# Attention in head pairs with transposed scores, and an MLP whose matmuls are issued between the attention phases

## The chip, the cores and the metric

The kernel runs on one core of a Trainium2 chip. The metric is the device time of one execution in microseconds (us), the median of three runs.

## The reference, cut to what matters

Attention over q, k, v of shape 8 batches x 8 heads x 576 positions x 64, then an MLP on the 4608 resulting tokens of width 512 with a hidden width of 2048.

```python
q_d, k_d, v_d = (t.reshape(B, H, 144, 4, D).mean(axis=3) for t in (q, k, v))
out_up = np.repeat(sm_attn(q_d, k_d, v_d), 4, axis=2)      # softmax over 144 groups
scores = np.where(np.abs(pos[:, None] - pos[None, :]) < 4, q @ k.T / 8, -1e9)
out_local = softmax(scores) @ v                            # a band of 7 positions
x = (out_up + out_local).transpose(0, 2, 1, 3).reshape(4608, 512)
h = x @ w_in                                               # 512 -> 2048
out = (h * sigmoid(h)) @ w_out                             # 2048 -> 512
```

## The kernel before

The program has two blocks, one after the other. The first does the attention, one head at a time, 64 times. Five engines each run a list of their own in order, tied together by counted semaphores (`Edge`). GpSimd (`g_D`, L442) loads q and k of two heads by a DMA that converts to bf16; SyncE (`sp_V`, `sp_W`, L449 to L460) loads v twice, once in plain rows and once in the five windows of the band. TensorE's list for a head is `pe_T` (transposes of q and k, L193 to L201; averages over groups of four by a matmul with `G_bf`, L206 to L222), `pe_D` and `pe_Dd` of the head before (transposing the normalised weights P, L256 to L268), `pe_S` and `pe_Sd` (scores, queries on the output's partitions, L236 to L244), `pe_O` and `pe_Od` of the head before (weights times v, L281 to L290). ScalarE does the exponentials (L305, L306, L314) and half of the copies out of PSUM (L324, L331, L353); VectorE multiplies by the band mask and sums each row (L377), takes reciprocals, scales the weights (L387), copies, and adds the two attention results into `xT` (L418, L423), which holds all 4608 tokens as 128 x 4 x 4608 in f32.

The second block begins when the last head is in `xT`. For each of nine groups of 512 tokens, `gemm1` makes 16 tiles of the hidden layer, four 128x512 matmuls each (L691), into two PSUM tiles; ScalarE takes the sigmoid (L676, SBUF), VectorE multiplies it by the PSUM tile (L650) into `gT` in bf16, and this frees the PSUM tile. `gemm2` of the group before follows as one run of 64 matmuls (L706); VectorE copies each of its four outputs (L659) and SyncE stores it.

A tile of `gemm1` may begin only when the tile two steps ago has been multiplied:

```python
eMG.wait(t, gch - 1)
```

Of the kernel before, what the change touches and what calls it, by code (L numbers as in the profile page):

```python
# [17 lines left out]
NCH = 5
QB = [0, 120, 240, 360, 480]  # L20
NQ = [120, 120, 120, 120, 96]
SK0 = [0, 117, 237, 357, 448]
MASK_IDX = [0, 1, 1, 1, 2]
MASK_OFF = [0, -3, -32]
# [2 lines left out]
NEG = -1.0e9


class Edge:  # L30

    def __init__(self, kctx, nc, name, dma=False):
        self.sem = kctx.enter_context(nc.semaphore(name))
        self.step = 16 if dma else 1
        self.n = 0

    def inc(self, inst):
        inst.then_inc(self.sem, self.step)
        self.n += 1
        return self.n  # L40

    def wait(self, eng, k):
        if k >= 1:
            eng.wait_ge(self.sem, self.step * k)  # L44


def bass_hourglass_attn__then__act_silu_kernel(
# [11 lines left out]
    with kctx:
        E = kctx.enter_context  # L60

        xT = E(nc.sbuf_tensor("xT", [128, 4, NTOK], F32))
# [12 lines left out]
        eDK = [edge(f"dk{i}", dma=True) for i in range(2)]
        eDV = [edge(f"dv{i}", dma=True) for i in range(2)]
        eDW = [edge(f"dw{i}", dma=True) for i in range(2)]
        eTq = edge("tq")
        eTk = edge("tk")
        ePvd = edge("pvd")  # L80
        ePs = edge("ps")
        ePsd = edge("psd")
        ePd = edge("pdg")
        ePdd = edge("pdd")
        ePo = edge("po")
        ePod = edge("pod")
        eDv = edge("dvcast")
        eXq = edge("xq")
        eXk = edge("xk")
# [34 lines left out]
        G64_bf = pa(nc.sbuf_tensor("G64_bf", [128, 16], BF16))
        Gf = pa(nc.sbuf_tensor("Gf", [128, 32], F32))
        w_out_st = pa(nc.sbuf_tensor("w_out_st", [128, 16, 512], F32))
        qkst = [pa(nc.sbuf_tensor(f"qkst{i}", [128, 9, 2 * D_], BF16)) for i in range(2)]
        vst = [pa(nc.sbuf_tensor(f"vst{i}", [128, 5, D_], F32)) for i in range(2)]
        wbst = [pa(nc.sbuf_tensor(f"wbst{i}", [128, NCH, D_], F32)) for i in range(2)]
        vbf = [pa(nc.sbuf_tensor(f"vbf{i}", [128, 5, D_], BF16)) for i in range(2)]  # L130
        wbf = [pa(nc.sbuf_tensor(f"wbf{i}", [128, NCH, D_], BF16)) for i in range(2)]
        qT_sb = [pa(nc.sbuf_tensor(f"qT{i}", [D_, S_], BF16)) for i in range(2)]
        kT_sb = [pa(nc.sbuf_tensor(f"kT{i}", [D_, S_], BF16)) for i in range(2)]
        qdT_sb = [pa(nc.sbuf_tensor(f"qdT{i}", [D_, SD], BF16)) for i in range(2)]
        kdT_sb = [pa(nc.sbuf_tensor(f"kdT{i}", [D_, SD], BF16)) for i in range(2)]
        P_sb = [pa(nc.sbuf_tensor(f"P{i}", [120, 640], BF16)) for i in range(2)]
# [609 lines left out]
```

## Time and profile before

| | |
|---|---|
| median of 3 runs (lowest to highest) | 718.29 us (716.72 to 719.34) |
| span of the profiled execution, first to last instruction | 715.0 us |
| median less that span | 3.3 us |
| busy: TensorE matmul, weight load | 623.9 us, 394.2 us |
| busy: VectorE, ScalarE, GpSimd | 452.8, 306.7, 71.4 us |
| attention block, to the first MLP matmul | 402.6 us |
| MLP block | 312.4 us |

For the profiled execution the page has the span and no other time; what lies around it is read as the 3.3 us by which the median is longer. A busy TensorE is not one at its peak: its matmuls overlap, and the share says nothing of the clock.

### The profile page before, as it was taken

The numbers are of one execution on the slowest core, as the hardware profiler recorded it, in microseconds if no ns is written. First come the engines' busy times: TensorE is split into PE (matmuls) and PEld (weight loads), VectorE is DVE, ScalarE is ACT, GpSimd is POOL, SyncE is SP. The second block draws the span as 40 slices with busy tenths as digits, with TensorE's granted clock in tenths as the row PEclk, the third lists the DMA queues.
The fourth block names the chain that finished last, engine by engine and source line by source line (L and its number), as shares of the span: only waits on it lengthen the run. The fifth ranks groups of instructions, "written<-read, shape, count | busy, mean of one in ns | idle before, by whom it ended". The sixth has DMA issues, their size and how long they took to land. (4 is left out here: it accounts for less than half of the span.)

```text
span 715.0 us, 12541 instructions
## 1 busy us (share of the span) xinstructions
PE 623.9 (87%) x3887; PEld 394.2 (55%) x3904; DVE 452.8 (63%) x1979; ACT 306.7 (43%) x978; POOL 71.4 (10%) x92
## 2 busy tenths in 40 slices
PE   1866979999999999999999688989898988989898
PEld 0544656666666666666666455455545555454543
DVE  1755999888888988889898455253434343343431
ACT  0543645666555566665556344141323222232310
POOL 5111112112121211212120000000000000000000
DMA  5998847576766757577671000101010101000012
GB/s 50 236 279 155 91 66 87 71 88 76 88 79 86 88 72 87 75 89 82 83 90 28 2 0 1 59 1 59 1 60 14 46 15 45 29 30 30 30 44 74
DMA packets 167586, 48.02 MB, mean 67 GB/s; under 512 B 160352, under 2 KB 160352, under 8 KB 167008
## 3 DMA queue, kind: packets, MB, share of 16 engines
q0 software_dynamic: 75280, 13.64, 22.2%
q1 hardware_dynamic: 92240, 33.59, 18.9%
q8 instruction: 32, 0.52, 0.3%
q14 instruction: 34, 0.28, 0.1%
HBM read 47.19 MB, written 9.44 MB: 79 GB/s over the span
## 5 line engine op out<-in xcount | busy, mean ns | idle before, releaser
L691 PE MATMUL hT<-xT,w_in_sb 128*128 128x512 f32 x576 | 155.2, 412 | 34.1 <-DVE gT L650 32.0
L676 ACT ACTIVATE sig<-hT 128x512 bf16<-128x512 f32 x144 | 85.9, 597 | 192.6 <-PE hT L691 192.6
L650 DVE TENSOR_TENSOR gT<-hT,sig 128x512 bf16<-128x512 f32 x144 | 99.5, 692 | 91.5 <-ACT sig L676 91.5
L691 PEld LDWEIGHTS hT<-xT,w_in_sb 128*128 128x128 f32 x576 | 99.6, 190 | 87.4 <-DVE gT L650 70.1
L706 PE MATMUL oT<-w_out_bf,gT 128*128 128x512 bf16 x559 | 123.4, 379 | 1.0
L353 ACT ACTIVATE kT<-ps 64x576 bf16<-64x576 bf16 x64 | 41.2, 644 | 149.1 <-PE ps L222 149.1
L706 PEld LDWEIGHTS oT<-w_out_bf,gT 128*128 128x128 bf16 x576 | 55.7, 98 | 68.3 <-issue 2.2
L377 DVE CUSTOM_DVE_ANT_0 P<-P,mask_bf 120x128 bf16<-120x128 bf16 (+1 forms) x320 | 72.7, 286 | 26.3 <-ACT P L306 25.9
L659 DVE COPY osb<-oT 128x512 f32<-128x512 f32 x36 | 24.9, 692 | 94.5 <-PE oT L706 94.5
L442 POOL DMA_DIRECT2D qkst<-in_q_dram x32 | 33.0, 1030 | 298.3 <-PE ps L222 297.5
L281 PE MATMUL ps<-PhT,wbf 128*64 128x120 bf16 (+1 forms) x320 | 42.3, 298 | 23.4 <-DVE xT L423 20.0
L387 DVE TENSOR_SCALAR P<-P,Z 120x128 bf16<-120x128 bf16 (+1 forms) x320 | 58.2, 251 | 2.2
L193 PE MATMUL ps<-id_bf,qkst 128*64 128x128 bf16 x256 | 40.6, 314 | 13.5 <-DVE vst L515 13.5
L236 PE MATMUL ps<-kT,qT 64*120 64x128 bf16 (+1 forms) x320 | 50.3, 318 | 2.2 <-ACT kT L353 2.2
L281 PEld LDWEIGHTS ps<-PhT,wbf 128*64 128x64 bf16 x320 | 30.8, 161 | 34.2 <-issue 33.2
L256 PE MATMUL ps<-id_bf,P 120*128 120x120 bf16 (+1 forms) x320 | 42.2, 297 | 7.1 <-DVE P L387 7.1
L418 DVE TENSOR_TENSOR xT<-ps,odT 64x480 fp32r<-64x480 f32 x64 | 41.6, 650 | 7.4 <-DVE odT L406 0.9
L324 ACT ACTIVATE PhT<-ps 128x480 bf16<-128x480 f32 x64 | 36.5, 571 | 11.9 <-PE ps L268 9.1
L201 PE MATMUL ps<-id_bf,qkst 128*64 128x128 bf16 x256 | 40.5, 314 | 0.0
L305 ACT ACTIVATE P<-ps 120x512 bf16<-120x512 f32 x64 | 38.2, 597 | 1.6 <-PE ps L244 0.8
L236 PEld LDWEIGHTS ps<-kT,qT 64*120 64x120 bf16 (+1 forms) x320 | 36.6, 204 | 3.8 <-issue 2.3
L193 PEld LDWEIGHTS ps<-id_bf,qkst 128*64 128x64 bf16 x256 | 25.2, 158 | 19.5 <-DVE vst L515 13.5
(84 smaller groups left out, 824.8 us busy)
## 6 DMA issues: line engine op xcount, KB each, us to landing
wbst<-in_v_dram SPq DMA_DIRECT2D x320, 32.0 KB, 2.0
out_dram<-osb SPq DMA_DIRECT2D x36, 256.0 KB, 2.0
vst<-in_v_dram SPq DMA_DIRECT2D x64, 128.0 KB, 2.5
qkst<-in_q_dram POOLq DMA_DIRECT2D x32, 144.0 KB, 4.0
qkst<-in_k_dram POOLq DMA_DIRECT2D x32, 144.0 KB, 5.1
w_in_sb<-in_moe_w_in_dram POOLq DMA_DIRECT2D x1, 4096.0 KB, 16.2
w_out_st<-in_moe_w_out_dram SPq DMA_DIRECT2D x1, 4096.0 KB, 15.3
vst<-in_v_dram SPq DMA_DIRECT2D x64, 16.0 KB, 2.7
```

Source lines behind the costliest of these rows:

```text
L193: last = t.transpose(dst[:, c * 128:(c + 1) * 128], stage[:, c, half], id_bf[:, :])
L236: last = t.matmul(out_, lhsT, rhs, start=True, stop=True)
L256: last = t.matmul(out_, lhsT, rhs, start=True, stop=True)
L281: last = t.matmul(out_, lhsT, rhs, start=True, stop=True)
L353: last = sc.activation(kT_sb[sl][:, :], kT_ps[:, :], AF.Copy)
L377: last = dve.tensor_tensor_reduce(blk_, blk_, mask_bf[0:NQ[c], mi, :], scale=1.0, scalar=0.0, op0=ALU.mult, op1=ALU.add, accum_out=Z_sb[sl ...
L387: last = dve.tensor_scalar_mul(blk_, blk_, Z_sb[sl][0:NQ[c], c:c + 1])
L418: dve.tensor_tensor(dst0, PS6[0:D_, 0:480], odT_sb[sl][:, 0:120].unsqueeze(2).to_broadcast([D_, 120, 4]), ALU.add)
L650: m = dve.tensor_tensor(gT[js][:, f, :], hT_ps[gch % 2][:, :], sig_sb[gch % 2][:, :], ALU.mult)
L676: a = sc.activation(sig_sb[gch % 2][:, :], hT_ps[gch % 2][:, :], AF.Sigmoid)
L691: last = t.matmul(hT_ps[gch % 2][:, :], w_in_sb[:, kc, 128 * f:128 * f + 128], xT[:, kc, cols].bitcast(F32R), start=(kc == 0), stop=(kc == 3))
L706: last = t.matmul(oT_ps[u % 2][:, :], gT[js][:, f, 128 * tt:128 * tt + 128], w_out_bf[:, f, :], start=(f == 0), stop=(f == 15))
```

## The change

The five lists are now made by one program-order list of operations (`P.op`), which derives the waits from named buffers. Attention runs over 32 pairs of heads. Both heads of a pair lie side by side: q and k are loaded in f32 by SyncE as 96-row chunks, converted by GpSimd (`cast`, 2 copies of 96x768; `castv`, a copy of 128x640 and two adds of 72x512 to 72x256 for the grouped v), and transposed together, so that head 0 is in partitions 0 to 63 and head 1 in 64 to 127. Scores are made with keys on the output's partitions, so that the weights need no transposing; the mask is one multiply of 128x1152 on VectorE (`do_mask`); the sums of two pairs come from matmuls with a matrix of ones (`ph_Z`), pass through SBUF by a DMA, a reciprocal, a DMA to DRAM and broadcast DMAs back (`do_recip`), and multiply the output of `ph_PV` out of PSUM (128x456 and 128x264). `do_add` (128x576) writes into `xT`, now a ring of 2048 tokens. Sum, reciprocal and product of a pair come up to three iterations after its scores (`LAG`).

PSUM is four tiles of one bank for the MLP (`hps`, `ops`) and two of two banks (`duo`) that the attention phases take in turns. `fill(n)` issues up to n pieces of the MLP list, each of four 128x512 matmuls; a first-layer piece of group j waits, in the program's order, for 4j+4 pairs to be done. The sigmoid is replaced by (1 + tanh(h/2)) h, with the factor 1/2 in the copy of the output, which moves from VectorE to ScalarE. The weights of the second layer are converted by their DMA. Loads per pair: two DMAs of 1152 pieces of 256 B (q, k), two of 640 (v in windows), one of 288 pieces of 1 KB.

```diff
-                gemm1(0)
-                for j in range(1, NSUP):
-                    gemm1(j)
-                    gemm2(j - 1)
-                gemm2(NSUP - 1)
...
+def ph_T(p):
+    D, bk = next_duo()
+    j = p % 2
+    for x, (nm, st, xt, xd) in enumerate((("q", qb, qT, qd), ("k", kb, kT, kd))):
+        tps = D[:, x, 0:288].bitcast(BF16)
+        dps = D[:, x, 288:432]
+        for c in range(6):
+            P.op("PE", lambda t, c=c, st=st, tps=tps: t.transpose(
+                tps[:, 96 * c:96 * c + 96], st[j][:, c, :, :].rearrange("p h d -> p (h d)"),
+                id_bf[:, :]), r=[R("id"), R(f"{nm}b{j}")], w=[bk[x]])
+        for c in range(6):
+            mm(dps[:, 24 * c:24 * c + 24], st[j][:, c, :, :].rearrange("p h d -> p (h d)"),
+               G_bf[:, :], [R("G"), R(f"{nm}b{j}")], [bk[x]])
...
+def ph_S1(p):
+    D, bk = next_duo()
+    j, m = p % 2, p % NP_
     for c in range(4):
+        for h in range(2):
+            rows = slice(64 * h, 64 * h + 64)
+            mm(D[:, h, QB[c]:QB[c] + NQ[c]], kT[j][rows, W0[c]:W0[c] + 128],
+               qT[j][rows, QB[c]:QB[c] + NQ[c]], [R(f"kT{j}"), R(f"qT{j}")], [bk[h]])
+    P.op("ACT", lambda e: e.activation(Pt[m][:, :, 0:456], D[:, :, 0:456], AF.Exp, scale=0.125),
+         r=bk, w=[R(f"P{m}")])
+def ph_S2(p):
+    D, bk = next_duo()
+    j, m = p % 2, p % NP_
+    for h in range(2):
+        rows = slice(64 * h, 64 * h + 64)
+        mm(D[:, h, 0:120], kT[j][rows, 448:576], qT[j][rows, 456:576],
+           [R(f"kT{j}"), R(f"qT{j}")], [bk[h]])
+    for s in range(2):
+        for h in range(2):
+            rows = slice(64 * h, 64 * h + 64)
+            mm(D[0:72, h, 120 + 144 * s:264 + 144 * s], kd[j][rows, 72 * s:72 * s + 72],
+               qd[j][rows, :], [R(f"kd{j}"), R(f"qd{j}")], [bk[h]])
+    P.op("ACT", lambda e: e.activation(Pt[m][:, :, 456:576], D[:, :, 0:120], AF.Exp, scale=0.125),
+         r=bk, w=[R(f"P{m}")])
+    P.op("ACT", lambda e: e.activation(
+        Pd[m][:, :, :, :].rearrange("p h s n -> p h (s n)"), D[0:72, :, 120:408],
+        AF.Exp, scale=0.125), r=bk, w=[R(f"Pd{m}")])
...
+def ph_Z(z):
+    D, bk = next_duo()
+    i = z % 2
+    prs = (2 * z, 2 * z + 1)
+    rr_ = [R("ones")] + [R(f"P{p % NP_}") for p in prs] + [R(f"Pd{p % NP_}") for p in prs]
+    hd = [(32 * (2 * a + h), prs[a] % NP_, h) for a in range(2) for h in range(2)]
+    for o, m, h in hd:
+        mm(D[o:o + 32, 0, 0:360], ones_bf[:, :], Pt[m][:, h, 0:360], rr_, [bk[0]])
+    for o, m, h in hd:
+        mm(D[o:o + 32, 1, 0:216], ones_bf[:, :], Pt[m][:, h, 360:576], rr_, [bk[1]])
+    for s in range(2):
+        for o, m, h in hd:
+            mm(D[o:o + 32, 1, 216:360], fours_bf[:, :], Pd[m][:, h, s, :], rr_, [bk[1]],
+               start=(s == 0), stop=(s == 1))
+    P.op("ACT", lambda e: e.activation(zc[i][:, :, :], D[:, :, 0:360], AF.Copy),
+         r=bk, w=[R(f"zc{i}")])
+    zsrc = zc[i][:, :, :].rearrange("p a n -> p (a n)")
+    for o in range(4):
+        P.op("SP", lambda s, o=o: s.dma_start(
+            zr[i][10 * o:10 * o + 10, :], zsrc[32 * o:32 * o + 1, :].rearrange("p (c n) -> p c n", c=10)),
+            r=[R(f"zc{i}")], w=[R(f"zr{i}")], dma=f"zr{i}")
+def do_recip(z):
+    i = z % 2
+    P.op("DVE", lambda e: e.reciprocal(rr[i][:, :], zr[i][:, :]), r=[R(f"zr{i}")], w=[R(f"rr{i}")])
+    P.op("SP", lambda s: s.dma_start(
+        scr[i].rearrange("h (c n) -> (h c) n", c=10), rr[i][:, :]),
+        r=[R(f"rr{i}")], w=[R(f"scr{i}")], dma=f"scr{i}")
+    for a in range(2):
+        n = (2 * z + a) % NR
+        for h in range(2):
+            P.op("SP", lambda s, a=a, h=h, n=n: s.dma_start(
+                Rb[n][64 * h:64 * h + 64, :],
+                scr[i][2 * a + h:2 * a + h + 1, :].to_broadcast([64, 720])),
+                r=[R(f"scr{i}")], w=[R(f"Rb{n}")], dma=f"Rb{n}")
...
+def ph_PV(p):
+    D, bk = next_duo()
+    m, n, u, x = p % NP_, p % NVB, p % NR, p % 2
+    b, kc = divmod(p, 4)
+    def pv(c):
+        for h in range(2):
+            o = (D[64 * h:64 * h + 64, 0, QB[c]:QB[c] + NQ[c]] if c < 4
+                 else D[64 * h:64 * h + 64, 1, 0:120])
+            mm(o, vb[n][:, 5 * h + c, :], Pt[m][:, h, QB[c]:QB[c] + NQ[c]],
+               [R(f"P{m}"), R(f"vb{n}")], [bk[0] if c < 4 else bk[1]])
+    for c in range(5):
+        pv(c)
+    for s in range(2):
+        for h in range(2):
+            mm(D[64 * h:64 * h + 64, 1, 120:264], vd[n][:, 2 * h + s, :], Pd[m][:, h, s, :],
+               [R(f"Pd{m}"), R(f"vd{n}")], [bk[1]], start=(s == 0), stop=(s == 1))
+    P.op("DVE", lambda e: e.tensor_tensor(xo[x][:, 0:456], D[:, 0, 0:456], Rb[u][:, 0:456], ALU.mult),
+         r=[bk[0], R(f"Rb{u}")], w=[R(f"xo{x}")])
+    P.op("DVE", lambda e: e.tensor_tensor(xo[x][:, 456:720], D[:, 1, 0:264], Rb[u][:, 456:720], ALU.mult),
+         r=[bk[1], R(f"Rb{u}")], w=[R(f"xo{x}")])
...
+def g1(j, f):
+    n = ng1[0]
+    ng1[0] += 1
+    hb, tb = n % 2, n % 2
+    t0 = (512 * j) % XR
+    for kc in range(4):
+        mm(hps[hb][:, :], w_in_sb[:, kc, 128 * f:128 * f + 128],
+           xT[:, kc, t0:t0 + 512].bitcast(F32R),
+           [R("w_in")] + xblk(kc, 512 * j, 512 * j + 512), [R(f"h{hb}", True)],
+           start=(kc == 0), stop=(kc == 3))
+    P.op("ACT", lambda e: e.activation(th[tb][:, :], hps[hb][:, :], AF.Tanh, scale=0.5),
+         r=[R(f"h{hb}", True)], w=[R(f"th{tb}")])
+    P.op("DVE", lambda e: e.scalar_tensor_tensor(
+        gT[j % 2][:, f, :], th[tb][:, :], 1.0, hps[hb][:, :], ALU.add, ALU.mult),
+        r=[R(f"h{hb}", True), R(f"th{tb}")], w=[R(f"g{j % 2}_{f}")])
+def g2(j, i):
+    tt, part = divmod(i, 4)
+    ob = (4 * j + tt) % 2
+    for f in range(4 * part, 4 * part + 4):
+        mm(ops[ob][:, :], gT[j % 2][:, f, 128 * tt:128 * tt + 128], w_out_bf[:, f, :],
+           [R("w_out"), R(f"g{j % 2}_{f}")], [R(f"o{ob}", True)],
+           start=(f == 0), stop=(f == 15))
+    if part == 3:
+        s_ = (4 * j + tt) % 2
+        row = 512 * j + 128 * tt
+        P.op("ACT", lambda e: e.activation(osb[s_][:, :], ops[ob][:, :], AF.Copy, scale=0.5),
+             r=[R(f"o{ob}", True)], w=[R(f"osb{s_}")])
+        P.op("SP", lambda s: s.dma_start(out[row:row + 128, :], osb[s_][:, :]),
+             r=[R(f"osb{s_}")], dma=f"os{s_}")
+mlp = []
+for j in range(NSUP):
+    for i in range(16):
+        mlp.append(("g1", j, i))
+        if j >= 1:
+            mlp.append(("g2", j - 1, i))
+mlp += [("g2", NSUP - 1, i) for i in range(16)]
+done_pairs = [0]
+def fill(n):
+    while n and mlp:
+        what, j, i = mlp[0]
+        if what == "g1" and done_pairs[0] < 4 * min(j, 7) + 4:
+            return
+        mlp.pop(0)
+        (g1 if what == "g1" else g2)(j, i)
+        n -= 1
+LAG = 3
...
+for it in range(NPAIR + LAG):
+    if it < NPAIR:
+        ph_T(it)
+        if it + 1 < NPAIR:
+            cast(it + 1)
+            castv(it + 1)
+        if it + 2 < NPAIR:
+            load(it + 2)
+        fill(2)
+    if it >= 2 and it % 2 == 0 and it // 2 - 1 < NPAIR // 2:
+        ph_Z(it // 2 - 1)
+        fill(1)
+    if it < NPAIR:
+        ph_S1(it)
+        fill(2)
+        ph_S2(it)
+        do_mask(it)
+        fill(2)
+    if it % 2 == 0 and it >= 2:
+        do_recip(it // 2 - 1)
+    if it >= LAG:
+        ph_PV(it - LAG)
+        fill(1)
+        do_add(it - LAG)
+        done_pairs[0] = it - LAG + 1
+        fill(1)
+fill(1000)
```

## Rows read from the trace of the kernel before

**Rows 1.** Windows by stage: us, busy us (instructions) of PE, PEld, DVE, ACT, POOL.
```profile
13.40:62.00 48.60, 33.02 (x262) 22.41 (x262) 26.51 (x150) 20.87 (x76) 6.77 (x7) 1.00 1.02 241
62.00:402.60 340.60, 314.76 (x2490) 216.50 (x2490) 301.11 (x1644) 198.64 (x758) 54.83 (x54) 1.00 0.62 77
...
444.40:478.30 33.90, 30.36 (x126) 17.11 (x128) 13.83 (x20) 9.52 (x17) 0.00 (x0) 1.00 0.08 31
```

**Rows 2.** Timeline of PE in one head: start, us, line, form, count.
```profile
203.92 0.29 PE L206 MATMUL ps<-G_bf,qkst 128*128 128x32 bf16 x4
204.15 0.19 PE L208 MATMUL ps<-G_bf,qkst 64*128 64x16 bf16 x1
...
204.60 0.66 PE L256 MATMUL ps<-id_bf,P 120*128 120x120 bf16 x5
205.06 0.31 PE L262 MATMUL ps<-id_bf,PdA 128*128 128x128 bf16 x1
...
205.73 0.79 PE L236 MATMUL ps<-kT,qT 64*120 64x128 bf16 x5
206.31 0.32 PE L242 MATMUL ps<-kdT,qdT 64*128 64x144 bf16 x1
...
206.92 0.66 PE L281 MATMUL ps<-PhT,wbf 128*64 128x120 bf16 x5
207.38 0.32 PE L288 MATMUL ps<-PdT,Vd 128*64 128x144 bf16 x1
```

**Rows 3.** Timeline of PE's weight loads in the same head.
```profile
202.98 0.13 PEld L195 LDWEIGHTS ps<-id_bf,qkst 64*64 64x64 bf16 x1 [0.17 <-issue]
```

**Rows 4.** Costliest groups by line: busy us, mean ns of one, idle before.
```profile
L676 ACT ACTIVATE sig<-hT 128x512 bf16<-128x512 f32 x144 | 85.9, 597 | 192.6 <-PE hT L691 192.6
...
L650 DVE TENSOR_TENSOR gT<-hT,sig 128x512 bf16<-128x512 f32 x144 | 99.5, 692 | 91.5 <-ACT sig L676 91.5
...
L418 DVE TENSOR_TENSOR xT<-ps,odT 64x480 fp32r<-64x480 f32 x64 | 41.6, 650 | 7.4 <-DVE odT L406 0.9
...
L193 PE MATMUL ps<-id_bf,qkst 128*64 128x128 bf16 x256 | 40.6, 314 | 13.5 <-DVE vst L515 13.5
...
L346 DVE COPY qT<-ps 64x576 bf16<-64x576 bf16 x64 | 28.3, 442 | 1.2 <-PE ps L222 1.0
...
L306 ACT ACTIVATE P<-ps 96x128 bf16<-96x128 f32 x64 | 16.8, 263 | 0.0
...
L195 PE MATMUL ps<-id_bf,qkst 64*64 64x64 bf16 x64 | 16.6, 260 | 0.0
...
L423 DVE TENSOR_TENSOR xT<-ps,odT 64x96 fp32r<-64x96 f32 x64 | 15.3, 240 | 0.0
...
L490 POOL CAST mask_bf<-maskf 120x128 bf16<-120x128 f32 x3 | 0.9, 291 | 0.2
...
L498 POOL CAST G_bf<-Gf 128x32 bf16<-128x32 f32 x1 | 0.2, 211 | 0.1
```

**Rows 5.** First MLP matmuls, by source line, in 403.6 to 405.
```profile
L691 PE MATMUL hT<-xT,w_in_sb x5: 628/628/628, 403.2 to 404.9; 128*128 128x512 f32 x5
```

**Rows 6.** The same line in 409 to 410.
```profile
L691 PE MATMUL hT<-xT,w_in_sb x5: 388/389/395, 408.7 to 409.6; 128*128 128x512 f32 x5
```

**Rows 7.** Timeline of one pair of first-product groups, weight loads.
```profile
502.74 0.77 PEld L691 LDWEIGHTS hT<-xT,w_in_sb 128*128 128x128 f32 x4 [0.17 <-DVE gT L650]
```

**Rows 8.** Timeline of PE in the first layer.
```profile
501.81 2.14 PE L691 MATMUL hT<-xT,w_in_sb 128*128 128x512 f32 x8 [0.48 <-DVE gT L650]
```

**Rows 9.** Timeline of the end.
```profile
711.87 0.69 DVE L659 COPY osb<-oT 128x512 f32<-128x512 f32 x1 [2.76 <-PE oT L706]
```

**Rows 10.** DMA of 62 to 402.6: queue (packets, MB, share of 16 engines), issues.
```profile
q1 hardware_dynamic: 74802, 17.55, 25.0%
...
vst<-in_v_dram SPq DMA_DIRECT2D x55, 128.0 KB, 2.5
```

**Rows 11.** Timeline where the MLP begins.
```profile
405.08 1.28 ACT L676 ACT_TABLE_LOAD   x1 [5.30 <-PE hT L691]
```

More of the change, by code (lines that the diff above doesn't have):

```diff
@@ L15 @@
 DFF = 2048
-NHEAD = B_ * H_
 SD = S_ // 4
[L19 to L24, printed above, removed]
-NSUP = 9
[L27 to L44, printed above, removed]
+NPAIR = B_ * H_ // 2
@@ L75, in bass_hourglass_attn__then__act_silu_kernel @@
[L75 to L89, printed above, removed]
@@ L124, in bass_hourglass_attn__then__act_silu_kernel @@
[L124 to L130, printed above, removed]
@@ L131, in bass_hourglass_attn__then__act_silu_kernel @@
[L131 to L136, printed above, removed]
@@ L602, in bass_hourglass_attn__then__act_silu_kernel @@
-        phA.__exit__(None, None, None)
-        if xdbg is not None:
-            with nc.Block() as blk2:
-                @blk2.sync
-                def _(s):
-                    eXo.wait(s, nheads)
-                    dm = s.dma_start(xdbg.rearrange("(sl p) t -> p sl t", p=128),
-                                     xT[:, :, :])
-                    eDOUT.inc(dm)
-                    eDOUT.wait(s, 1)
-            return
-        gT = [E(nc.sbuf_tensor(f"gT{i}", [128, 16, 512], BF16)) for i in range(2)]
@@ new lines, in bass_hourglass_attn__then__act_silu_kernel, with R, sb @@
+        P = Prog()
+        res = {}
+        def R(name, psum=False):
+            if name not in res:
+                res[name] = Res(name, psum)
+            return res[name]
+        def sb(name, shape, dt, n=1):
+            ts = [E(nc.sbuf_tensor(f"{name}{i}", shape, dt)) for i in range(n)]
+            return ts if n > 1 else ts[0]
+        XR = 2048
+        w_in_sb = sb("w_in_sb", [128, 4, DFF], F32R)
+        w_out_bf = sb("w_out_bf", [128, 16, 512], BF16)
+        xT = sb("xT", [128, 4, XR], F32)
@@ new lines, in bass_hourglass_attn__then__act_silu_kernel @@
+        xo = sb("xo", [128, 720], F32, 2)
+        scr = [nc.dram_tensor(f"scr{i}", [4, 720], F32, kind="Internal").ap() for i in range(2)]
+        id_bf = sb("id_bf", [96, 96], BF16)
+        G_bf = sb("G_bf", [96, 24], BF16)
+        mask_bf = sb("mask_bf", [128, S_], BF16)
+        ones_bf = sb("ones_bf", [128, 32], BF16)
+        fours_bf = sb("fours_bf", [72, 32], BF16)
+        cf = xo[1]
+        duo = [E(nc.psum_tensor(f"duo{i}", [128, 2, 512], F32)) for i in range(2)]
+        hps = [E(nc.psum_tensor(f"hps{i}", [128, 512], F32)) for i in range(2)]
@@ new lines, in bass_hourglass_attn__then__act_silu_kernel, with pool @@
+        ops = [E(nc.psum_tensor(f"ops{i}", [128, 512], F32)) for i in range(2)]
+        W0 = [112 * c for c in range(5)]
+        QB = [0, 120, 232, 344, 456]
+        NQ = [120, 112, 112, 112, 120]
+        def pool(fn, r=(), w=()):
+            return P.op("POOL", fn, r, w)
+        c0 = R("xo1")
+        pool(lambda g: g.memset(cf[0:96, 0:96], 0.0), w=[c0])
+        pool(lambda g: g.affine_select(out=cf[0:96, 0:96], in_=cf[0:96, 0:96], compare_op=ALU.not_equal,
+                                       fill=1.0, base=0, pattern=[[-1, 96]], channel_multiplier=1),
+             r=[c0], w=[c0])
```

791 lines of the change are left out of this document (238 added, 553 removed).

## The prediction

> **What bounds the kernel now.** I read the busy time by stage first, then TensorE's timeline inside one head and inside the MLP, then the durations by form. From 62 to 402.6 us TensorE is busy 314.8 of 340.6 us and VectorE 301.1 [rows 1], so the attention block is TensorE's, with VectorE close behind. In the MLP a group of 512 tokens takes 33.9 us, of which TensorE is busy 30.4 [rows 1]. The reader is to see that neither number says that TensorE works at its rate. In the MLP a first-layer tile of four matmuls occupies it for 0.77 + 0.17 = 0.94 us [rows 7], but pairs of tiles follow each other more slowly: sigmoid 0.60 and multiply 0.69 [rows 4] stand in the way of the next tile, with two PSUM tiles only, and TensorE idles 0.48 us a pair [rows 8]. The second layer runs without gaps: sixteen matmuls take 2.76 + 0.69 = 3.45 us, 0.216 each [rows 9]. So 16 x 0.94 + 64 x 0.216 = 28.9 us of the 33.9 is work, and the nine groups are worth 260 of the block's 312 us.
>
> In the attention block the point is TensorE's clock. The granted clock reads 1.00 (2.4 GHz) in every stretch, the third number from the right in [rows 1], but durations contradict it. The first MLP matmuls, right behind the attention, took 628 ns and followed each other at (404.9 - 403.2)/4 = 0.43 us [rows 5]; four us later, after eight of them back to back, the same form took 389 ns, at 0.225 us [rows 6]. The difference, 239 ns for 512 columns, is about that between 1.2 and 2.4 GHz (0.833 and 0.417 ns a column: 213). Attention matmuls lengthen by (314 - 260)/64 = 0.84 ns a column [rows 4]: that block ran at 1.2 GHz. Its engine is "busy" 92% of the time with short matmuls at half rate, and none of the 512-column ones lies among them.
>
> **The change, part by part.** TensorE first, for one pair of heads, at the low level, from steps between starts [rows 2]. A 120-column matmul with 128 weights takes (205.06 - 204.60)/5 = 0.092 us, so 96 columns 0.072; a 32-column one (204.15 - 203.92)/4 = 0.058; a score matmul (206.31 - 205.73)/5 = 0.116; a matmul with v (207.38 - 206.92)/5 = 0.092; 144 columns I take at 0.13.
> - Transposes and group means: 12 x 0.072 + 12 x 0.058 = 1.56.
> - Scores: 8 x 0.116 + (2 x 0.116 + 4 x 0.13) = 1.68.
> - Products with v: 10 x 0.092 + 4 x 0.13 = 1.44.
> - Sums: 16 matmuls per two pairs, 3456 columns, 2.88 us one after the other, or a quarter if the four column tiles run together: 1.44 or 0.36 a pair; I take 0.9.
> - Changes of tile shape: before one, the weight load waits 0.17 us [rows 3]. Seven in a pair with MLP pieces between the phases: 1.2.
>
> That is 6.8 us a pair, against twice (402.6 - 13.4)/64 = 6.1 for two heads before. At the high level 6,624 columns lose 0.417 ns each, 2.8 us at most, so 4.0 to 6.8; much of a short step is not columns, and I take 5.3.
>
> How the changes are priced rests on the 0.17 us seen between short matmuls. The Trainium skill (TensorEngine Tiling (Array Packing), Key Properties) says that a change of tiling mode drains the engine. Behind a 512-column matmul a drain costs more than here, by 389 - 225 = 164 ns [rows 6]: by that rule 7 x 0.16 = 1.1 us more for each interleaved pair, some 28 us in all, 533 instead of 505. No trace here has such a switch.
>
> An MLP piece costs 0.94 (first layer) or 0.86 (second). An iteration with interleaving issues eight on average, four of each: 7.2 us. During it the other engines do, with line slopes of (597 - 263)/384 = 0.87 ns a column on ScalarE, (650 - 240)/384 = 1.07 on VectorE, (291 - 211)/96 = 0.83 on GpSimd [rows 4]:
> - ScalarE: copies 0.65 + 0.28, exponentials 0.95 + 0.36 + 0.65, sums 0.39, and 4 tanh and one output at 0.60: 6.3 us.
> - VectorE: 0.44 + 0.29, mask 1152 columns (0.7 to 1.4), products 0.62 + 0.42, add 0.75, reciprocal 0.1, 4 multiplies at 0.69: 6.4.
> - GpSimd: 0.82 + 0.82 + 0.72, the two adds between one and two times 1.0: 3.4 to 4.4.
> - DMA: 3,872 packets at 25.0% x 16 x 340.6/74802 = 18 ns on 16 engines [rows 10]: 4.4.
>
> All are under half of TensorE's 12.5, which covers them. What hid tanh and multiply badly before (a tile of two steps ago) is now hidden by the second-layer pieces and phases between. I add 0.5 us for waits: 13.0. If the cover fails, tanh and multiply show again, as in rival 2.
>
> Now the order of issue, counted from `fill`. Nothing is interleaved in iterations 0 to 6, since four pairs must be done, three iterations late. 15 first-layer pieces go into iterations 7 and 8; 9 and 10 are nearly empty, until pair 8 is done; 11 to 31 hold 168 pieces, eight each; 32 to 34 seven. 96 (40 first, 56 second) remain behind the attention. The sum:
> - Start to the first transposes: 13.4 before, most of it constants on GpSimd; now only the identity, the loads by SyncE and two casts: 10. The later constants delay the second cast by some 3.
> - Iterations 0 to 6 at the low level: 6.8 less three changes of shape, 6.3; evictions can't be hidden by MLP pieces, so a wait of about 2.2 between phases: 7 x 8.5 = 60. Two weight transfers of 4 MB share the DMA engines with the loads: from 13.4 to 62 us TensorE had 48.6 - 33.0 = 15.6 idle [rows 1]; I take 8.
> - Iterations 7 and 8: 2 x 6 + 15 x 0.94 = 26; 9 and 10: 17.
> - Iterations 11 to 31: 21 x 13.0 = 273.
> - 32 to 34: seven pieces 6, sums and products 5, and the last reciprocal, whose chain of three transfers (zr, scr, Rb) at about 2.5 us [rows 10] has little work before it: 5. Together 16.
> - The remaining pieces: 40 x 0.94 + 56 x 0.86 = 86. From the last copy's start to the end 715.0 - 711.9 = 3 [rows 9].
>
> 10 + 3 + 60 + 8 + 26 + 17 + 273 + 16 + 86 + 3 = 502 as a span. The profiled span before was 715.0, and the median 718.3 lies 3.3 above it: 505 us.
>
> SyncE's queue is where a late step is next seen. Behind the wait for a reciprocal stand its DRAM write, the four broadcasts, and the next pair's five loads; a pair's loads are issued two iterations ahead, so that 10 us of delay there cost nothing in an interleaved iteration. VectorE waits in order for the reciprocal's input, a transfer of some 2.5 us [rows 10]; five MLP pieces lie between, but in the empty iterations nothing does (in the 2.2 us above).
>
> **The rivals.**
> 1. Small tiles run at once. The two heads' scores use different rows of the array, sums and products different columns. If all did, the 5.3 would lose about 1 us: 33 pairs make 33 us, 472. No row of before shows two tiles at once; 12%.
> 2. Waits in in-order queues. If an interleaved iteration is 2.5 to 3.5 us longer, since multiplies queue behind the mask and behind products that wait for a broadcast, and the empty ones 2 us, 21 x 3 + 9 x 2 = 81: 586, or 560 to 600. For it speaks that pairs of tiles stalled 0.48 us in the MLP before [rows 8]; against it, that half of each engine is free. 17%.
> 3. Tanh and exp need different tables. A table load took 1.28 us where the sigmoid began [rows 11]. Four switches an iteration, 23 iterations: 118 us of ScalarE, which rises to 11.4 of 13 us, so that most of it shows: about 590. The Trainium skill (ScalarE: Activation LUTs, Table sets) puts the two in one set, by which no load would come; before has no tanh. 4%.
> 4. The other side, and the change not doing what it says: short matmuls between pieces keep TensorE at 1.2 GHz. A piece then costs 4 x 0.43 = 1.72, 0.8 more, on 288 pieces 235 us, and pairs stay at 6.8, 1.5 more in 22: 268 in all, 773. It is slower than before once 213 of these 268 are paid, four fifths of the pieces. For it speaks that the clock was low through all the attention; against it, that it rose within eight MLP matmuls, stayed up through the 0.48 us gaps of the first layer, and that the 96 pieces at the end are unmixed. All: 4%; a third to a half of the pieces (600 to 640): 6%.
>
> **How the numbers follow.** The sum as it stands, 57%: 505, itself between 475 (pairs at 4.0, no waits) and 550 (6.8 and the drain). The range takes in rival 1 and most of rival 2: 462 to 595. What is outside, rivals 3 and 4 and the tails, has under 2 in 10. Within 0.3% is about what a measurement of this kernel can't tell from no change; 1%. Slower 5%, from rival 4 whole or nearly; faster 94%.
>
> **What would show it.** Right: 512-column matmuls at 0.22 us among the attention phases, short matmuls there that lengthen by about 0.42 ns a column, one table load in all, iterations 11 to 31 of about 13 us, a start of about 80 us before the first tanh, and some 90 us of MLP alone at the end. Wrong: 628 ns matmuls amid the iterations; TensorE waiting on VectorE's multiply or the products; VectorE on the broadcasts; many table loads; or GpSimd's casts as the last wait of the transposes.

## Result and the profile after

The changed kernel takes 483.67 us (median of 4 runs, 482.44 to 490.62) against 717.69 us beside it: a ratio of 0.673, 95% interval 0.672 to 0.675. The highest of the four runs was in a slower state of the chip and is left out of the ratio. The profiled execution has a span of 480.7 us.

By stage: iterations 0 to 6, 7 and 8, 9 and 10, iterations 11 to 30, and the pieces behind the attention. Columns as in [rows 1].

```profile
5.21:95.36 90.15, 25.97 (x375) 19.51 (x375) 18.58 (x36) 20.07 (x38) 45.44 (x64) 1.00 0.94 200
95.36:119.50 24.14, 23.19 (x181) 15.27 (x181) 15.28 (x24) 14.93 (x27) 6.41 (x7) 1.00 0.72 133
119.50:144.04 24.54, 8.80 (x128) 6.13 (x125) 9.82 (x18) 6.08 (x12) 11.23 (x13) 0.60 0.63 131
144.04:365.32 221.28, 207.86 (x1841) 121.56 (x1841) 123.17 (x214) 117.73 (x210) 85.44 (x95) 0.96 0.76 164
392.90:480.70 87.80, 84.61 (x376) 47.70 (x374) 27.40 (x40) 31.66 (x53) 0.00 (x0) 0.99 0.15 54
```

Where MLP pieces lie between the phases, TensorE is busy 94 to 96%. Where almost none do (first and third row) it is busy 29 and 36%, GpSimd, the busiest engine, 50 and 46%, and 115 us pass. The DMA share, the second number from the right, is 0.94 and 0.63 there.

TensorE's timeline through one interleaved pair (form of [rows 2]):

```profile
202.33 0.43 PE L300 MATMUL duo<-Pt,ones_bf 128*32 128x360 bf16 x8
202.58 0.30 PE L300 MATMUL duo<-Pd,fours_bf 72*32 72x144 bf16 x8
202.81 1.04 PE L300 MATMUL ops<-w_out_bf,gT 128*128 128x512 bf16 x4
203.78 0.37 PE L300 MATMUL duo<-qT,kT 64*128 64x120 bf16 x8
204.09 1.19 PE L300 MATMUL hps<-xT,w_in_sb 128*128 128x512 f32 x4
...
206.10 0.23 PE L300 MATMUL duo<-qT,kT 64*128 64x120 bf16 x2
206.16 0.29 PE L300 MATMUL duo<-qd,kd 64*72 64x144 bf16 x4
206.38 1.21 PE L300 MATMUL hps<-xT,w_in_sb 128*128 128x512 f32 x4
...
208.40 0.44 PE L300 MATMUL duo<-Pt,vb 128*64 128x120 bf16 x10
208.68 0.29 PE L300 MATMUL duo<-Pd,vd 72*64 72x144 bf16 x4
208.90 1.20 PE L300 MATMUL hps<-xT,w_in_sb 128*128 128x512 f32 x4
...
210.81 0.42 PE L310 MATMUL duo<-id_bf,qb 96*128 96x96 bf16 x6
...
211.63 1.18 PE L300 MATMUL hps<-xT,w_in_sb 128*128 128x512 f32 x4
```

Read starts, not durations: the eight large sums have (202.58 - 202.33) = 0.25 us from their first start to the next row's, and 2304 columns; one 512-column matmul takes 0.225 [rows 6]. From start to start the sums of two pairs take 0.48 us, a pair's scores 0.31 and 0.28, its products 0.50, its transposes and means 0.82: 2.15 a pair with half the sums.

ScalarE and VectorE in the costliest groups by line (as [rows 4] and [rows 11]): tanh, gating product, the only table load, and the reciprocal.

```profile
L453 ACT ACTIVATE th<-hps 128x512 f32<-128x512 f32 x144 | 86.0, 597 | 152.9 <-PE hps L300 152.7
...
L455 DVE SCALAR_TENSOR_TENSOR gT<-th,hps 128x512 bf16<-128x512 f32 x144 | 98.9, 687 | 149.0 <-ACT th L453 148.6
...
L322 ACT ACT_TABLE_LOAD x1 | 1.3, 1283 | 0.8 <-PEq L545 0.8
...
L387 DVE RECIPROCAL rr<-zr 40x72 f32<-40x72 f32 x17 | 10.1, 593 | 62.5 <-DMA zr<-zc 62.5
```

The unmixed iterations are explained by SyncE's own queue; its timeline in iterations 4 to 6, where the second column is the time that the issues hold the queue:

```profile
59.88 1.92 SPq L269 DMA_DIRECT2D vs<-in_v_dram  x2
61.85 0.62 SPq L271 DMA_DIRECT2D vq<-in_v_dram  x1
62.51 0.44 SPq L262 DMA_DIRECT2D qs<-in_q_dram  x1
62.99 1.27 SPq L262 DMA_DIRECT2D ks<-in_k_dram  x1
64.31 3.10 SPq L269 DMA_DIRECT2D vs<-in_v_dram  x2
67.45 0.65 SPq L271 DMA_DIRECT2D vq<-in_v_dram  x1
68.14 3.04 SPq L381 DMA_DIRECT2D zr<-zc  x4
73.46 0.32 SPq L388 DMA_DIRECT2D scr<-rr  x1
74.75 2.43 SPq L394 DMA_DIRECT2D Rb<-scr  x4
```

and VectorE and ScalarE, from their timelines there:

```profile
60.91 0.77 ACT L377 ACTIVATE zc<-duo 128x720 f32<-128x720 f32 x1 [1.66 <-PE duo L300]
...
72.83 0.60 DVE L387 RECIPROCAL rr<-zr 40x72 f32<-40x72 f32 x1 [8.54 <-DMA zr<-zc]
...
74.96 0.45 DVE L317 COPY qT<-duo 128x576 bf16<-128x576 bf16 x1
```

The sums are in SBUF at 61.7. Their four transfers stand behind the loads of two pairs, are issued from 68.1 to 71.2, and have landed by 72.8. VectorE waits 8.5 us for them in order, and behind the reciprocal stands the copy of the next pair's q (L317), without which TensorE can make no scores. In the chain that ended last the longest piece is a load, and it is late for another reason, the traffic of the weights:

```profile
16.40 1.15 POOL w_out_bf L502
...
19.17 25.05 DMA ks<-in_k_dram
```

Right behind the issue of the two weight transfers, the load of one pair's k (288 KB, 6.3 us at the median) took 25 us. Behind it in SyncE's queue the issue of two loads took 17 us, where two such issues take 1.92 and 3.10 above:

```profile
21.00 17.09 SPq L269 DMA_DIRECT2D vs<-in_v_dram  x2
```

The interleaved iterations have one wait as well. The first first-layer piece of a new group of tokens needs the last of four pairs in `xT`, and stands directly behind the addition that puts it there. So TensorE waits once in every fourth iteration, at 188.3, 231.6, 275.7, 321.8 and 365.0 us, 13.4 us in all; the longest:

```profile
275.73 0.79 PE L300 MATMUL hps<-xT,w_in_sb 128*128 128x512 f32 x1 [4.02 <-DVE xT L435]
```

### The profile page after: what moved, and what is told of

Its sections match the earlier page's. It is cut to its first block, busy times and chain, and to the rows that moved or that the text cites. A ratio compares the mean times of both kernels' runs of the same rounds, so it can differ in the third digit from the quotient of the medians.

```text
span 480.7 us, 7698 instructions
## 1 busy us (share of the span) xinstructions
PE 374.1 (78%) x3072; PEld 223.4 (46%) x3072; DVE 208.3 (43%) x361; ACT 201.5 (42%) x357; POOL 150.2 (31%) x187
## 4 chain that ended last, share of the span: by engine, by line
PE 65%; DMA 14%; SPq 7%; DVE 5%; POOL 4%; issue 3%; ACT 2%; POOLq 0%; ACTq 0%
PE hps L300 29%; PE ops L300 25%; PE duo L300 8%; DMA ks<-in_k_dram 5%; DMA zr<-zc 4%; SPq L381 4%; PE duo L310 3%; DMA vq<-in_v_dram 2%; DVE xT L435 2%; SPq L269 2%; DMA Rb<-scr 1%; DVE xo L417 1%; ACT th L453 1%; DMA scr<-rr 1%; POOL kb L278 1%
## 5 line engine op out<-in xcount | busy, mean ns | idle before, releaser
L300 PE MATMUL hps<-xT,w_in_sb 128*128 128x512 f32 x576 | 188.0, 448 | 37.3 <-DVE xT L435 32.6
L455 DVE SCALAR_TENSOR_TENSOR gT<-th,hps 128x512 bf16<-128x512 f32 x144 | 98.9, 687 | 149.0 <-ACT th L453 148.6
L300 PE MATMUL ops<-w_out_bf,gT 128*128 128x512 bf16 x576 | 151.2, 391 | 0.0
L453 ACT ACTIVATE th<-hps 128x512 f32<-128x512 f32 x144 | 86.0, 597 | 152.9 <-PE hps L300 152.7
L300 PEld LDWEIGHTS hps<-xT,w_in_sb 128*128 128x128 f32 x576 | 108.2, 198 | 74.7 <-DVE xT L435 36.2
L300 PEld LDWEIGHTS ops<-w_out_bf,gT 128*128 128x128 bf16 x576 | 46.7, 99 | 65.9 <-issue 26.1
L322 ACT ACTIVATE kT<-duo 128x576 bf16<-128x576 bf16 x32 | 20.8, 651 | 57.9 <-PE duo L300 57.9
L286 POOL TENSOR_TENSOR vt<-vq 72x512 f32<-72x512 f32 x32 | 41.1, 1286 | 6.8 <-DMA vq<-in_v_dram 6.6
L335 ACT ACTIVATE Pt<-duo 128x912 bf16<-128x912 f32 x32 | 29.7, 929 | 28.5 <-PE duo L300 28.5
L300 PE MATMUL duo<-qT,kT 64*128 64x112 bf16 (+1 forms) x320 | 20.0, 236 | 25.5 <-DVE qT L317 21.3
L387 DVE RECIPROCAL rr<-zr 40x72 f32<-40x72 f32 x17 | 10.1, 593 | 62.5 <-DMA zr<-zc 62.5
L310 PE MATMUL duo<-id_bf,qb 96*128 96x96 bf16 x192 | 16.5, 233 | 25.5 <-POOL qb L278 25.5
L278 POOL CAST kb<-ks 96x768 bf16<-96x768 f32 x32 | 28.2, 882 | 25.3 <-DMA ks<-in_k_dram 24.7
L435 DVE TENSOR_TENSOR xT<-xo 128x576 fp32r<-128x576 f32 (+4 forms) x40 | 30.7, 783 | 0.6
L288 POOL TENSOR_TENSOR vd<-vt 72x256 bf16<-72x256 f32 x32 | 24.5, 766 | 4.3
```

What stands on the lines that cost most here:

```text
L278: pool(lambda g, a=a, bb=bb: g.tensor_copy(bb[j][:, :, :, :], a[i][:, :, :].rearrange("p (h c) d -> p c h d", h=2)), r=[R(f"{nm}s{i}")], w ...
L286: pool(lambda g: g.tensor_tensor(vt[:, :, :], vq[i][:, :, 0:128], vq[i][:, :, 128:256], ALU.add), r=[R(f"vq{i}")], w=[R("vt")])
L288: pool(lambda g: g.tensor_tensor(vd[m][:, :, :], vt[:, :, 0:64], vt[:, :, 64:128], ALU.add), r=[R("vt")], w=[R(f"vd{m}")])
L300: return P.op("PE", lambda t: t.matmul(out_, lhsT, rhs, start=start, stop=stop, skip_group_check=True), r, w)
L310: P.op("PE", lambda t, c=c, st=st, tps=tps: t.transpose(tps[:, 96 * c:96 * c + 96], st[j][:, c, :, :].rearrange("p h d -> p (h d)"), id_bf ...
L335: P.op("ACT", lambda e: e.activation(Pt[m][:, :, 0:456], D[:, :, 0:456], AF.Exp, scale=0.125), r=bk, w=[R(f"P{m}")])
```

## Experiments

Times are medians; ratios are to the kernel before, with 95% intervals. Unless said otherwise each edit is made to the changed kernel alone.

### Where the gain comes from: pieces in bursts, and the old attention with its pieces taking turns

```diff
         def fill(n):
+            if n < 100:
+                return
...
                 done_pairs[0] = it - LAG + 1
-                fill(1)
+                if it % 4 == 2:
+                    fill(1000)
```

> The MLP pieces are no longer put between the phases of attention: after every fourth iteration all that are ready are issued in one run. Theory: the gain of mixing is that pieces fill TensorE's waits and keep its clock up; without it four iterations cost about 9.8 us each as in the starved ones, and 32 pieces 29 us, so 68 us in place of 44 for each of six groups: 600 to 640. Rival: the gain is in the cheaper attention work alone, and the order of the pieces is worth little: 484 to 520.

621.22 us, ratio 0.869 (0.865 to 0.874). The kernel before with first- and second-layer pieces taking turns, as the changed kernel's do:

```diff
-                gemm1(0)
-                for j in range(1, NSUP):
-                    gemm1(j)
-                    gemm2(j - 1)
-                gemm2(NSUP - 1)
...
+                for j in range(NSUP):
+                    for i in range(16):
+                        gemm1(j, i)
+                        if j >= 1:
+                            gemm2(j - 1, i)
+                for i in range(16):
+                    gemm2(NSUP - 1, i)
```

(`gemm1` and `gemm2` now make one tile and a quarter of an output tile; VectorE's copies of the output stand after every fourth multiply.)

> The kernel before with one part of the change alone: in its MLP block a first-layer tile and a quarter of a second-layer tile take turns. Theory: the stall of 0.48 us per pair of tiles is hidden by the second-layer pieces, 33.9 us per group become 28.9: 312 become 262 to 270 and the whole 668 to 677. Rival: the multiply is still late for the next tile, as the copies of the output stand in the same VectorE queue: 700 to 718.

676.85 us, ratio 0.944 (0.942 to 0.946). So 40 us of the 234 are to be had in the old MLP by order alone, and in the new kernel interleaving with the attention is worth 621 - 484 = 137: without it the attention stalls on its transfers, and in part at the low clock as well. How much of the 137 is either, no run separates. The bursts are seen in the page's 40 slices of that run (TensorE's busy tenths, its granted clock in tenths):

```profile
PE   1312246753983479644982389643983698399997
...
PEclk9999999955995579755995579755995599589999
```

### Rival 1: do tiles run at once?

A tile is here the part of TensorE's rows or columns that a small matmul uses. First by the order of issue, so that neighbours use the same tile:

```diff
-            for c in range(4):
-                for h in range(2):
+            for h in range(2):
+                for c in range(4):
                     rows = slice(64 * h, 64 * h + 64)
```

(likewise for the other scores, sums and products.)

> The loops over the two heads (and over the four column tiles of the sums) are turned round, so that neighbouring small matmuls use the same part of the array; the work is the same. Theory: in the changed kernel neighbours on different parts ran at once, and this made a pair cheap. In its trace, at 2.4 GHz, eight score matmuls took 0.31 us where 912 columns alone need 0.38, and the fourteen products 0.50 where 1728 columns need 0.72. One after the other a pair then costs 0.8 to 1.2 us more, 17 to 25 us over the 21 mixed iterations: 500 to 509 us. Rival: the step is set by the issue of an instruction and not by the array, so the order doesn't matter: 481 to 487.

484.38 us, ratio 0.677 (0.673 to 0.682): no difference from the change. It would be wrong to conclude that tiles don't run at once. This program issues, for one column tile after the other, two large sums and two small ones. In its timeline all eight large sums nevertheless start before the first small one, and have 203.06 - 202.80 = 0.26 us to the next row's start:

```profile
202.80 0.46 PE L300 MATMUL duo<-Pt,ones_bf 128*32 128x360 bf16 x8
203.06 0.33 PE L300 MATMUL duo<-Pd,fours_bf 72*32 72x144 bf16 x8
203.32 1.04 PE L300 MATMUL ops<-w_out_bf,gT 128*128 128x512 bf16 x4
```

The large sums of the last tile start ahead of the small ones of the first, which were issued before them: the order of issue is not the order of work. The edit had not taken away what it was to test. So the tiles themselves were made one:

```diff
-                    rows = slice(64 * h, 64 * h + 64)
+                    rows = slice(0, 64)
...
-                mm(D[o:o + 32, 0, 0:360], ones_bf[:, :], Pt[m][:, h, 0:360], rr_, [bk[0]])
+                mm(D[0:32, 0, 0:360], ones_bf[:, :], Pt[m][:, h, 0:360], rr_, [bk[0]])
```

(likewise for the other scores and sums, and the products.)

> The changed kernel with the tiles that lie side by side put into one: both heads' scores take rows 0 to 63 (head 0's scores twice), the sums of all four heads and the products of both are written into the first column tile, so that the other partitions keep old values. The number and size of the matmuls stay. Theory (matmuls in different tiles run at once in the changed kernel: eight sums of 2304 columns took 0.25 us, where one of 512 columns takes 0.225): a pair then costs 0.417 ns for each of 1728 columns of sums, 1728 of products and 1728 of scores, 2.16 us instead of the 0.24 + 0.50 + 0.59 read from the trace, 0.8 us more, for some 25 pairs 20 us: 497 to 510 us. Rival (they follow one another in either layout and the short steps are only in the records): 481 to 488 us.

504.45 us, ratio 0.703 (0.699 to 0.707): 20.8 us more, as the theory had it. Its timeline:

```profile
210.56 1.16 PE L300 MATMUL duo<-Pt,ones_bf 128*32 128x360 bf16 x8
211.55 0.67 PE L300 MATMUL duo<-Pd,fours_bf 72*32 72x144 bf16 x8
212.37 0.81 PE L300 MATMUL ops<-w_out_bf,gT 128*128 128x512 bf16 x3 [0.16 <-issue]
213.12 0.57 PE L300 MATMUL duo<-qT,kT 64*128 64x120 bf16 x8
213.62 1.20 PE L300 MATMUL hps<-xT,w_in_sb 128*128 128x512 f32 x4
...
228.65 0.69 PE L300 MATMUL duo<-Pt,vb 128*64 128x120 bf16 x10
229.18 0.41 PE L300 MATMUL duo<-Pd,vd 72*64 72x144 bf16 x4
229.53 1.20 PE L300 MATMUL hps<-xT,w_in_sb 128*128 128x512 f32 x4
```

The eight large sums now take 0.99 us to the next row instead of 0.25 (2304 columns at 0.417 ns are 0.96), all sixteen 1.81 instead of 0.48 to the first recorded matmul of the next piece (of whose four one is missing in the trace, about 0.2 us), the first scores 0.50 instead of 0.31, the products 0.88 instead of 0.50. An iteration without waits takes 1.28 us more: 13.03 and 10.57 us in turn (from 207.85), 11.80 on average, against 10.52 in the changed kernel.

### Is TensorE the bound of the interleaved iterations?

```diff
-                for c in range(6):
+                for c in (0, 1, 2, 3, 4, 5) * 2:
                     P.op("PE", lambda t, c=c, st=st, tps=tps: t.transpose(
```

> The changed kernel with each of the twelve 96-column transposes of a pair issued twice. Theory (TensorE sets the time of the mixed iterations 11 to 31 and of little before): six transposes took 0.26 us from the first start to the next phase, so 0.5 us more a pair, for some 24 pairs 12 us, 492 to 500 us. Rival (another engine or a queue sets the mixed iterations too, and TensorE's 93% busy is only long matmuls waiting): 481 to 488 us.

491.43 us, ratio 0.686 (0.683 to 0.689): 7.8 us, of the 12 expected and just short of the theory's range. From iteration 11's first transpose to iteration 31's it takes 226.8 us instead of 221.3, so 0.28 a pair out of 0.52 added. Iterations without a wait lengthen by nearly all of it, from 11.20 and 9.84 us to 11.70 and 10.34 (from 207.34); in the others the wait for `xT` takes up the extra work. TensorE sets the pace where it doesn't wait.

### Rival 3: the price of tables

```diff
-            P.op("ACT", lambda e: e.activation(th[tb][:, :], hps[hb][:, :], AF.Tanh, scale=0.5),
+            P.op("ACT", lambda e: e.activation(th[tb][:, :], hps[hb][:, :], AF.Sigmoid),
```

(and the product and the copy without their constants.)

> Sigmoid times h in place of (1 + tanh(h/2)) h, with the factor 1/2 dropped. Theory: tanh shares the table of the exponential and sigmoid doesn't, so that ScalarE loads tables about four times in each of some 24 iterations, 1.28 us each, 100 loads and 120 us of ScalarE, and the score and tanh steps wait: 560 to 620 us. Rival: the table load hides under TensorE's 11 us an iteration, of which ScalarE used about 6: 484 to 510.

532.43 us, ratio 0.740 (0.735 to 0.745). The table loads, by line:

```profile
L453 ACT ACT_TABLE_LOAD x48 | 61.6, 1283 | 0.8
...
L335 ACT ACT_TABLE_LOAD x24 | 30.8, 1283 | 0.4
...
L350 ACT ACT_TABLE_LOAD x23 | 29.5, 1283 | 0.4
```

95 loads beside the first, 122 us of ScalarE, cost 48.8 us: between theory and rival. Some 60% of that time stays hidden.

### The unmixed iterations: attention alone, then the queue's order, the weights, and the number of transfers

```diff
-        for j in range(NSUP):
+        for j in range(7, NSUP):
...
-                if j >= 1:
+                if j >= 8:
```

> The MLP is left out for token groups 0 to 6 (their output isn't written); groups 7 and 8 follow the attention, 64 pieces, about 58 us. It gives the time of the attention when nothing is mixed in. Theory: it is bound by SyncE's queue, whose issues take about 17 us for two pairs, and by the sums that stand in it behind two pairs' loads: two iterations in 19 to 20 us, 35 in 330 to 350, and 395 to 420 in all, with VectorE waiting for the input of its reciprocal some 8 us every second iteration. Rival: TensorE at 1.2 GHz is the bound, about 5 us of work a pair with its waits of 2: 250 for the attention, 310 in all.

426.3 us, ratio 0.594 (0.593 to 0.595). Two pairs take 20.5 us on average over the window below (transposes of q start at 102.05, 122.62 and 143.18), and the whole lies 6 us above the theory's range; the rival's 310 fell. Windows and waits of that run:

```profile
102.05:347.80 245.75, 93.01 (x1486) 71.49 (x1484) 82.20 (x166) 71.22 (x133) 100.30 (x115) 1.00 0.79 153
```

```profile
DVE rr L387 <- DMA zr<-zc: 153.6, 16, 27.3
```

No compute engine is busy for half of the time (GpSimd 41%); 16 waits for the sums make 154 us. The DMA share is 0.79, more than that of any compute engine.

Loads issued behind the sums' transfers, and the weights in quarters over iterations 0 to 7:

```diff
-                if it + 2 < NPAIR:
-                    load(it + 2)
                 fill(2)
...
                 fill(1)
+            if it + 2 < NPAIR:
+                load(it + 2)
             if it < NPAIR:
                 ph_S1(it)
```

> The five loads of the pair two ahead are issued behind the transfers of the sums instead of ahead of them; nothing else changes. Theory (order): in the iterations without MLP pieces VectorE waits 8.5 us every second one for the input of the reciprocal, because the sums' transfers stand behind ten loads in SyncE's queue; there are four such waits, one of them 26 us with the weights' transfer in it. With the sums first most of it goes: 455 to 468 us. Rival (throughput): the queue is full with 17 us of issues for two pairs in 19.5 us, so that the wait only moves to the loads: 476 to 485.

468.25 us, ratio 0.654 (0.651 to 0.656), at the edge of the theory's range.

```diff
...
+        def weights(it):
+            if it < 4:
+                P.op("POOL", lambda g: g.dma_start(w_in_sb[:, it, :], wi[:, it, :]), w=[R("w_in")], dma="w_in")
...
```

> The two weight matrices come in quarters, one per iteration from 0 to 7, instead of whole at 15 us. Theory: the pair loads that waited 25 us behind 8 MB then wait little, and the gap of iterations 2 to 4 (22.6 to 57.0 us) shrinks from 34 to about 20: 465 to 473. Rival: the same bytes pass the same engines before the first MLP piece, so it only spreads: 479 to 487.

477.76 us, ratio 0.665 (0.661 to 0.669), between the two. Both edits:

> Both edits. If the two waits are different ones their gains add: 440 to 455 us. If both are the same full queue, it is no better than the better of the two.

464.25 us, ratio 0.648 (0.646 to 0.650): 19.4 us, nearly the sum of 15.4 and 5.9, but short of what was expected. Four transfers of sums as one, first with nothing else, then with both edits:

```diff
-            for o in range(4):
-                P.op("SP", lambda s, o=o: s.dma_start(
-                    zr[i][10 * o:10 * o + 10, :], zsrc[32 * o:32 * o + 1, :].rearrange("p (c n) -> p c n", c=10)),
-                    r=[R(f"zc{i}")], w=[R(f"zr{i}")], dma=f"zr{i}")
+            P.op("SP", lambda s: s.dma_start(
+                zr[i][0:40, :], zsrc[0:128:32, :].rearrange("p (c n) -> p c n", c=10)),
+                r=[R(f"zc{i}")], w=[R(f"zr{i}")], dma=f"zr{i}")
```

> The changed kernel with the four transfers zr of two pairs' sums as one, nothing else moved. With both waits moved the same edit gave 13.5 us. Theory (SyncE's queue is the bound of the unmixed iterations, so that any 2.4 us less of issue for two pairs shows there whatever the order): 468 to 475 us. Rival (the issues show only once the two pairs' loads no longer stand ahead of the sums): 479 to 487 us.

473.76 us, ratio 0.661 (0.659 to 0.662). The time lies in the theory's range, but the theory's place was wrong: of 9.1 us of span only 2.3 are gained ahead of iteration 11, 2.4 in iterations 11 to 30 and 4.4 behind the start of 31, where VectorE's wait for the last sums falls from 4.1 us to 1.9. In the unmixed iterations the shorter issue counts for little while two pairs' loads stand ahead of it, as the rival had it.

> The kernel with both waits moved (loads behind the sums' transfers, weights in quarters: 464.25 us) and the four transfers zr of two pairs' sums as one. Theory (SyncE's issue time is still on the path of the unmixed iterations): four zr issues took 3.04 to 3.12 us, one is estimated at 0.8, so 2.3 us less for two pairs in the some five unmixed double iterations, 452 to 460 us. Rival (the transfer's own latency and the wait for scr and Rb set these iterations, not the issues): 462 to 467 us.

450.72 us, ratio 0.629 (0.628 to 0.631): the fastest kernel here, 33 us under the change. The one issue held the queue for 0.59 us instead of 3.04. Read from TensorE's timelines (first transpose of an iteration), the spans, and VectorE's waits for zr (the sums) and for Rb (the broadcasts):

| kernel | iteration 0 | 11 | 31 | span | waits for zr, us | for Rb, us |
|---|---|---|---|---|---|---|
| the change | 5.2 | 144.0 | 365.3 | 480.7 | 62.5 | 6.7 |
| one transfer | 5.2 | 141.8 | 360.7 | 471.6 | 53.1 | 6.4 |
| weights late | 5.3 | 138.4 | 359.0 | 472.5 | 49.8 | 9.8 |
| sums first | 5.4 | 132.3 | 349.1 | 464.4 | 36.0 | 25.0 |
| both | 5.3 | 130.8 | 346.9 | 461.9 | 26.1 | 31.4 |
| both, one transfer | 5.5 | 120.7 | 334.1 | 445.1 | 15.9 | 22.0 |

Of the last one's 35.6 us of span, 23 are gained ahead of iteration 11 and 8 in iterations 11 to 30, which fall from 11.06 to 10.67 us each. With the same edit, "both" to "both, one transfer" gains 10.1 ahead of iteration 11. Moving the sums first takes 26.5 us off the waits for zr and adds 18.3 to those for Rb: part of the wait only moves on. All these runs move the same bytes, so order and number of transfers count by themselves. The DMA share stays high, though, and no run separates the queue's time from the load of the engines that move the bytes.

## Why the prediction was right, and where it was off

The direction, the range and the case (the sum as it stands) held; the time is 21 us under the forecast, and that it is so near is luck: two larger differences cancel.

| term | predicted | measured | difference |
|---|---|---|---|
| start to the first transposes | 10 | 5.2 | -5 |
| iterations 0 to 6, with the weights | 71 | 90.2 | +19 |
| 7 and 8 | 26 | 24.1 | -2 |
| 9 and 10 | 17 | 24.5 | +8 |
| 11 to 31 | 273 | 232.3 (21 x 11.06) | -41 |
| 32 to 34 | 16 | 16.5 | 0 |
| the rest | 89 | 87.8 | -1 |

**Mis-sized: the attention's columns at the high clock.** Iterations without a wait take 11.20 and 9.84 us in turn (first transposes at 155.24, 166.44 and 176.28), 10.52 on average. They hold nine pieces and eight, and others seven, so that four iterations have 32. Of the 10.52 the phases are 2.15; I had put 5.3, of which 1.2 for changes of tile shape, so 4.1. The 8.5 pieces take the other 8.4 us instead of the 7.6 that my prices give: the 0.7 that they lose by having phases between them stands in the place of the 1.2 put down for the changes. With eight pieces at this price, 7.9 us, and 2.15 for the phases, 1.0 of the average 11.06 is left, for which I had 0.5: the waits for `xT` are 0.67 an iteration, and behind some of them the granted clock falls (0.86 on average from 188 to 200 us). What was wrong in the 4.1 is two things. Sums, scores and products were let count nearly column by column: put into one tile, they cost 1.28 us a pair more, 3.4 in all. And I took only about half of what the clock gives ("much of a short step is not columns"). With all of it, and nothing side by side, my own steps come to an estimated 6.12 - 6,624 x 0.417 ns = 3.4 us, which is what the one-tile kernel has; the other 0.7 is this.

Rival 1's mechanism, given 12% as one that no row showed, is at work. Its price of 1 us a pair was low, and its sum of 33 us too high, since pairs outside the interleaved iterations wait anyhow: the one-tile kernel loses 20.8 us. Its 472 lies nearer than the forecast's 505.

The Trainium skill (TensorEngine Tiling (Array Packing), Key Properties) says that different tiles can load weights and multiply in parallel; the one-tile run agrees, with 0.99 us for the eight large sums that took 0.25. The drain at a change of mode, from the same list, by which the time would have been 533, shows no more than the 0.7 us an iteration.

**Mis-sized the other way: waits between unmixed phases.** I allowed 2.2 us an iteration and 8 for the weights, reasoning that a transfer of 2.5 us would be waited for. The transfer does take about that (2.3 from the start of the last of four issues). What I left out is the queue ahead of it: some 16 us of issues for two pairs on SyncE (the rows above, with the second pair's q and k). I had followed what stands behind the reciprocal's wait on SyncE, but not what stands ahead of the transfers that the reciprocal waits for, nor that on VectorE the next pair's copy of q stands behind it. These runs bear it out: attention alone at 20.5 us for two pairs; 15.4 us gained by order alone; 5.9 by the weights; 13.5 by three issues fewer with both moved. In the fastest kernel iterations 0 to 6 take 74.6 us and 9 and 10 take 18.2, near the 71 and 17 of the forecast. Three issues fewer alone gave 9.9, but mostly elsewhere. Whether the issues were long by themselves, or because the engines that move the bytes were loaded (DMA share 0.94 in iterations 0 to 6), stays open.

**Right:** the high clock among the phases ([rows 5] showed what the low one would look like; 512-column matmuls follow each other at 0.24 to 0.26 us between the phases), so rival 4 fell; in the bursts' run the granted clock did fall to 0.5 between them. TensorE as the bound where it doesn't wait (doubling the transposes: 0.50 us of 0.52 in such iterations, 7.8 of 12 us in all). Tanh and product hidden (TensorE waits 4.7 us for the product in all), so rival 2's place was wrong: its waits came, but mostly in the unmixed iterations. One table load in all; rival 3's 590 would have been 532. The Trainium skill (ScalarE: Activation LUTs, Table sets) has tanh in exp's set; the trace agrees, with one load for both. Two slips in the working change nothing: ScalarE's 6.3 and VectorE's 6.4 us are a little over half of 12.5, not under it, and there are 32 pairs, not 33.

What remains open: why both moved waits together gave no more than 19.4 us, where 29 to 44 were expected. The 29 to 44 supposed more than the two edits' own gains, whose sum is 21.3. In that run VectorE waits 31.4 us for the broadcasts and SyncE 65.2 for the write to DRAM before them, so the round trip itself seems to be next; no run removes it.

## What to carry to other kernels

Price a transfer by its queue: list what is issued ahead of it, with the time that each issue holds the queue, and then what stands behind the instruction that waits for it. Then look at where a gain came, not only at its size: the one transfer alone fell into its range for another reason. Small matmuls that use different rows or columns of TensorE cost nearer to the longest tile than to their sum, in both orders tried here; put them between long ones, and test it by making the tiles one, since reordering them tested nothing here. Count the pieces in an iteration before you call its rest a wait. When a forecast lands close, set its terms beside the stages: here errors of +27 and -49 us cancelled.
